# Scores by pairs of heads through a block-diagonal weight, and a fixed order of the first loads

## The chip, the cores and the metric

The kernel runs on one core of one Trainium2 chip. The metric is the device time of one execution in microseconds (us): 813.83 us is the median of three runs before the change (813.06 to 814.3). A core has a matrix engine (TensorE, PE in the profile, its weight loads PEld), three elementwise engines (VectorE is DVE, ScalarE is ACT, GpSimd is POOL) and SyncE (SP), which here only issues DMAs. Each engine runs its instructions in the order in which they were written for it, and waits at the first one whose inputs or buffer are not there. On-chip memory (SBUF) has 128 partitions; matmul results land in PSUM banks of 128 x 512 floats.

## The reference

There are 8 batches of 8 heads, 576 tokens, head width 64, and 32 memory slots per head. `phi` is `[8, 8, 576, 32]`.

```python
a   = softmax(phi, axis=2)                   # over the tokens
k_m = einsum('bhsm,bhsd->bhmd', a, k)        # 32 memory keys and values per head
v_m = einsum('bhsm,bhsd->bhmd', a, v)
scores = matmul(q, k_m^T) / sqrt(64)
x   = softmax(scores) @ v_m                  # then [8*576, 512]
out = relu(x @ w_in) ** 2 @ w_out            # 512 -> 2048 -> 512
```

All tensors are 32-bit floats, and the inputs q, k and phi are scaled so that the softmaxes are sharp; the kernel therefore keeps each large product as a sum of a high and a low part.

## The kernel before

**The work on one batch.** A batch is handled in two halves of four heads (`hh` = 0, 1). `memory(b, hh)` loads `phi`, k and v of four heads, takes the softmax over tokens, and multiplies into PSUM tile `pkv` (L426: four heads side by side, each in its own 32 columns of the array; 20 matmuls), sums (L439 for b < 2, L442 or L445 after that), and the reciprocal `rs`. From it come the transposed values `VTh`/`VTl` and the memory keys. `vw_step` and `vw_alone` multiply the values by w_in (`pvw`), so that `step` needs only the attention weights: `mm1` (L740) gives h, `mm2` (L770, L771, L773) multiplies the squared relu by w_out, and `mm2_left` (L796) does the last 64 tokens.

**Scores, batches 2 to 7.** `scores(b, hh)` loads q of two heads per DMA, 64 partitions of 18 x 64 floats (L557, two DMAs, 24 in all). The keys are scaled on ACT (`kvn`, L474), transposed 32 x 32 on DVE (`kT`, L477), and spread by a multiplication with the mask `bd` to a block weight `kb` of 2 x 128 columns (L562). q is transposed on DVE in two pieces of 8 and 10 token groups (`qT`, L569), and each piece is two matmuls over 128 partitions that add up in PSUM, one for each half of the head width (L574): 128 weights columns, 256 or 320 moving columns. DVE then transposes the scores back (L578), and the softmax follows.

**Scores, batches 0 and 1.** `first_attention` loads q by token rows (L602, 8 DMAs of 128 KB; the last 64 tokens by L595, tile `qx`), turns it on PE (L613), and multiplies by a block-diagonal key weight `kbd` of 128 x 128 (L636, L648). `kbd` comes from `kvx`, two DVE instructions (L459) that write keys and values twice beside each other under a parity mask, and a pair of PE transposes (L466).

**The weights.** w_in and w_out arrive as 64-bit pairs (`raw`, L322), are decoded to a high and a low part on DVE and ACT (L324 to L344) and for the first pieces on PE (`pd`, L350 to L352). w_in's parts are written to DRAM by POOL and loaded again as `wi` (L369) in later batches.

**What sets the order.** The kernel writes down all operations with an estimated duration on each engine they may use (`Plan.op`). `Plan.order` walks back from the due times of `mm2` (`cap`, set by `due`) to a latest start for each operation, and then fills the engines in time: an engine takes the ready operation whose latest start comes first, and preparatory work (`lead=True`) is taken 9 us (LEAD) ahead. The estimates also choose the engine where two are allowed. All loads go through one queue, SP. Of the loads of a batch the phi, k and v loads are two DMAs each (512 tokens, L377, and the last 64, L378).

## Time and profile before

| | |
|---|---|
| time, median of 3 (lowest, highest) | 813.83 us (813.06, 814.3) |
| the profiled execution: its own time; first to last instruction | 816.34 us; 814.6 us |
| PE busy | 776.2 us (95%) |
| DVE, ACT, POOL busy | 536.4, 403.1, 63.8 us |
| mean granted TensorE clock, first to last instruction | 0.994 |
| DMA packets, bytes | 99716, 101.04 MB |
| score matmuls L574, records and busy | 96, 27.6 us |

A row of a timeline has the start in us, the length, the engine, the line, the operation, the tile written and those read, and in brackets the idle time just before with what ended it. The length of a matmul includes its way through the array, so that lengths overlap: what a matmul takes from the next one is read from the starts. A 32-bit matmul of tiles that are not rounded appears as two records. A row of a table of windows has the stretch, its length, the busy time of PE, PEld, DVE, ACT and POOL with the number of instructions, the granted clock, the share of time that the DMA engines were busy and GB/s. SPq are the DMAs that SP issues.

### The profile page before, as it was taken

Reading aid. Unit: us, or ns where it says so; the run is one execution under the profiler, and the core shown is the slowest. Engines: PE = TensorE matmul, PEld = TensorE weight load, DVE = VectorE, ACT = ScalarE, POOL = GpSimd, SP = SyncE. Lnnn points to the kernel's source line nnn. Section 1 sums busy time; section 2 is a strip of 40 time slices with the busy share of each in tenths; the row PEclk is TensorE's granted clock in tenths of the full one; section 3 lists DMA queues with packets and bytes.
Section 4 is the critical chain, followed back from the end, with each engine's and each line's share of the span. In section 5 each row is a group of like instructions: output and inputs, shape, how many; then the busy total and the mean of one; then the engine's idle time right before and its main releaser. Section 6 shows DMA issues by size and latency. Waiting matters only on the chain.

```text
span 814.6 us, 13267 instructions
## 1 busy us (share of the span) xinstructions
PE 776.2 (95%) x4926; PEld 652.5 (80%) x4926; DVE 536.4 (66%) x1190; ACT 403.1 (49%) x922; POOL 63.8 (8%) x103
## 2 busy tenths in 40 slices
PE   4889999999999999999999999999999999999995
PEld 2567888778887888888778888888788888888884
DVE  4678888783468976766776556877677556864540
ACT  2557766675653465634445355644334355643220
POOL 4012202320100100010000100010000100000000
PEclk9999999999999999999999999999999999999998
DMA  7969967666456523423443433513422433100001
GB/s 225 270 191 286 270 176 239 188 170 191 125 146 189 165 81 105 129 37 90 132 125 88 126 106 104 136 34 91 133 58 70 122 108 104 30 24 29 1 1 64
DMA packets 99716, 101.04 MB, mean 124 GB/s; under 512 B 32260, under 2 KB 85508, under 8 KB 99652
## 3 DMA queue, kind: packets, MB, share of 16 engines
q1 hardware_dynamic: 89188, 81.55, 34.2%
q0 software_dynamic: 10464, 18.65, 8.8%
q8 instruction: 39, 0.64, 0.3%
q14 instruction: 25, 0.20, 0.1%
HBM read 79.17 MB, written 17.83 MB: 119 GB/s over the span
## 4 chain that ended last, share of the span: by engine, by line
PE 73%; DVE 8%; issue 6%; DMA 5%; ACT 4%; SPq 1%; POOL 1%; DVEq 0%; POOLq 0%; ACTq 0%
PE h L740 20%; PE acc L770 12%; PE acc L773 12%; PE acc L771 12%; PE accl L796 5%; PE pvw L536 4%; PE psc L574 3%; PE pkv L426 2%; DMA raw<-in_moe_w_out_dram 1%; DMA phi<-in_phi_dram 1%; ACT vw L260 1%; DMA raw<-in_moe_w_in_dram 1%; DMA wo<-work 1%; DVE glo L750 1%; DVE work L327 1%
## 5 line engine op out<-in xcount | busy, mean ns | idle before, releaser
L740 PE MATMUL h<-ath,vw 128*128 128x320 f32 (+1 forms) x1024 | 211.6, 298 | 1.1 <-ACT r L744 0.6
L770 PE MATMUL acc<-wo,gh 128*128 128x512 f32 x512 | 207.0, 404 | 1.8 <-ACT gh L746 1.6
L771 PE MATMUL acc<-wo,gh 128*128 128x512 f32 x512 | 201.7, 394 | 0.0
L740 PEld LDWEIGHTS h<-ath,vw 128*128 128x128 f32 x1024 | 171.0, 189 | 17.2 <-ACT r L744 1.7
L773 PE MATMUL acc<-wo,glo 128*128 128x512 f32 x512 | 162.1, 405 | 1.7 <-DVE glo L750 1.5
L260 ACT CAST vw<-pvw 64x256 fp32r<-64x256 f32 (+1 forms) x224 | 85.7, 397 | 74.5 <-PE pvw L536 35.4
L545 DVE TENSOR_TENSOR vw<-pvw,vw 64x256 fp32r<-64x256 f32 x192 | 78.8, 420 | 64.8 <-ACT vw L260 62.9
L770 PEld LDWEIGHTS acc<-wo,gh 128*128 128x128 f32 x512 | 96.4, 188 | 23.4 <-ACT gh L746 3.7
L740 PE MATMUL h<-atl,vw 128*128 128x320 f32 (+1 forms) x512 | 109.9, 295 | 0.0
L771 PEld LDWEIGHTS acc<-wo,gh 128*128 128x128 f32 x512 | 96.4, 188 | 16.6
L773 PEld LDWEIGHTS acc<-wo,glo 128*128 128x128 f32 x512 | 89.5, 189 | 19.5 <-DVE glo L750 6.2
L746 ACT ACTIVATE gh<-r 128x512 fp32r<-128x512 f32 x128 | 80.8, 632 | 43.4 <-DVE r L745 37.6
L750 DVE TENSOR_TENSOR glo<-r,gh 128x512 fp32r<-128x512 f32 x128 | 87.5, 684 | 21.4 <-ACT r L748 19.7
L744 ACT ACTIVATE r<-h 128x256 f32<-128x256 f32 (+1 forms) x149 | 60.1, 406 | 56.8 <-PE h L740 53.5
L745 DVE TENSOR_SCALAR r<-h 128x320 f32<-128x320 f32 (+1 forms) x107 | 48.9, 459 | 58.4 <-PE h L740 57.9
L740 PEld LDWEIGHTS h<-atl,vw 128*128 128x128 f32 x512 | 82.5, 189 | 0.7 <-issue 0.2
L747 ACT ACTIVATE gl<-r 128x64 fp32r<-128x64 f32 x128 | 32.8, 256 | 68.5 <-DVE r L745 66.5
L748 ACT ACTIVATE r<-r 128x576 f32<-128x576 f32 x94 | 64.5, 686 | 2.2
L796 PE MATMUL accl<-wo,gl 128*128 128x512 f32 x192 | 52.3, 397 | 0.1
L796 PEld LDWEIGHTS accl<-wo,gl 128*128 128x128 f32 x192 | 35.0, 188 | 7.2 <-DVE o L260 0.5
L536 PE MATMUL pvw<-wi,VTh 128*128 128x256 f32 x192 | 37.3, 286 | 0.6 <-issue 0.3
L749 DVE TENSOR_TENSOR r<-r 128x576 f32<-128x576 f32 x34 | 25.7, 756 | 15.8 <-ACT gh L746 14.4
(137 smaller groups left out, 854.3 us busy)
## 6 DMA issues: line engine op xcount, KB each, us to landing
wi<-w_in_hi SPq DMA_DIRECT2D x56, 256.0 KB
wi<-w_in_lo SPq DMA_DIRECT2D x56, 256.0 KB
KV<-in_k_dram SPq DMA_DIRECT2D x32, 256.0 KB
KV<-in_v_dram SPq DMA_DIRECT2D x32, 256.0 KB
raw<-in_moe_w_in_dram SPq DMA_DIRECT2D x16, 512.0 KB
raw<-in_moe_w_out_dram SPq DMA_DIRECT2D x16, 512.0 KB
q<-in_q_dram SPq DMA_DIRECT2D x24, 288.0 KB
out_dram<-o POOLq DMA_DIRECT2D x20, 256.0 KB, 7.7
```

The source lines that it names most:

```text
L260: nc.scalar.copy(o, i) if e == "ACT" else ENG[e].tensor_copy(o, i)
L536: nc.tensor.matmul(pw()[:, x * SL:(x + 1) * SL], l()[:, 2 * hh + x, :], w(r, x), start=(i == 0), stop=(i == 2))
L545: vec({"DVE": tt(SL)}, lambda e, V=V, pr=pr, src=src: nc.vector.tensor_sub(V()[pr, 1, hh, :], src(), V()[pr, 0, hh, :].bitcast(F32)), [pw, ...
L740: nc.tensor.matmul(p()[:, 0:n], V()[:, l, hh, c0:c0 + P], x()[:, hh, cs], start=(i == 0), stop=(i == 5))
L744: op({"ACT": act(n) - 30, **({} if b < 2 else {"DVE": tt(n)})}, lambda e, cs=cs, n=n, p=p: nc.scalar.activation(r()[:, cs], p()[:, 0:n], A ...
L746: op({"ACT": act(SM)}, lambda e: nc.scalar.activation(gh(), r()[:, 0:SM], AF.Square), [r], [gh])
L748: op({"ACT": act(S), **({} if b < 2 else {"DVE": tt(S)})}, lambda e: nc.scalar.activation(r(), r(), AF.Square) if e == "ACT" else nc.vecto ...
L750: vec({"DVE": tt(SM)}, lambda e: nc.vector.tensor_sub(glo(), r()[:, 0:SM], gh().bitcast(F32)), [r, gh], [glo])
L770: nc.tensor.matmul(a(), gh()[:, c], t()[:, 0], start=f0, stop=False)
L771: nc.tensor.matmul(a(), gh()[:, c], t()[:, 1], start=False, stop=False)
L773: nc.tensor.matmul(a(), glo()[:, c], t()[:, 0], start=False, stop=f1)
L796: nc.tensor.matmul(a(), G()[:, l, :], t()[:, w], start=(ff == 0 and n == 0), stop=(ff == NFF - 1 and n == 2))
```

## The change

It has two parts.

1. Batches 2 to 7 get their scores as the first two batches do, from a block-diagonal weight. `memory` now makes `kvx`, two PE transposes and `kbd` for every batch; the tiles `kvn`, `kT`, `vx` and `kb` and their instructions are gone. Each piece of q is still two matmuls, but one for each pair of heads: 64 weight columns, 256 or 320 moving columns, all 128 partitions, and the two stand in different halves of the array's columns (`tile_position=(0, 64 * y)`) and write different halves of the PSUM partitions. For that q must lie with two heads' halves of the head width on the partitions: each load now takes one head and half of its width, 32 x 18 pieces of 32 floats, eight DMAs in place of two (96 in place of 24). The planned durations of these steps are as before.
2. A list `FIRST` names the first loads in a fixed order, and gives each a `cap` far ahead of all others, so that the planner issues them in this order on SP.

```diff
+    def dma(fn, size, r=(), w=(), eng="SP", two=False, first=None, **more):
...
+        if first in FIRST:
+            more["cap"] = 10000 * FIRST.index(first) - 1e6
...
+    FIRST = ['phi 0 0', 'kv 0 0', 'phi 0 1', 'kv 0 1', 'wi 0', 'q 0 0', 'q 0 1', 'ql 0', 'wo 0']
...
-    kbd = kTs[b, hh] = st([P, P], F32, "kb", f"kbd{u}", 2)              # b < 2 only
+    kbd = kTs[b, hh] = st([P, P], F32, f"kb{b % 2}{hh}", f"kbd{u}")
...
-        Q = st([P, NC * D], F32, "q", f"q{u}")
-        for x in (0, 1):
-            h0 = 4 * hh + 2 * ((x + b) % 2)
-            dma(lambda d, x=x, h0=h0: d(Q()[64 * x:64 * x + 64], q[b, h0:h0 + 2].rearrange("h (p c) d -> (h p) (c d)", c=NC)),
-                2 * S * D * 4, [], [(Q, x)], lead=True)
+    def halves_of(d, dst, src):
+        for u in (0, 1):
+            d(dst[32 * u:32 * u + 32], src[:, 32 * u:32 * u + 32].rearrange("(p c) d -> p c d", c=NC))
...
+        Q = st([P, 2, NC, 32], F32, "q", f"q{u}")
+        for y in (0, 1):
+            for i in (0, 1):
+                hd = 4 * hh + (2 * (y + b) + i) % 4
+                dma(lambda d, y=y, i=i, hd=hd: halves_of(d, Q()[64 * i:64 * i + 64, y], q[b, hd]), S * D * 4, [], [(Q, (y, i))], two=True, lead=True)
...
-                for x in (0, 1):
-                    nc.tensor.matmul(pq()[:, 0:32 * n], kb()[:, x].rearrange("p h m -> p (h m)"),
-                                     qT()[:, x, 0:n].rearrange("p c t -> p (c t)"), start=(x == 0), stop=(x == 1))
+                for y in (0, 1):
+                    ys = slice(64 * y, 64 * y + 64)
+                    nc.tensor.matmul(pq()[ys, 0:32 * n], kbd()[:, ys], qT()[:, y, 0:n].rearrange("p c t -> p (c t)"),
+                                     start=True, stop=True, tile_position=(0, 64 * y))
```

The first place where rows move is SP's queue at the start of the program. The names are the tile and the tensor in DRAM that it is read from; `KV_1_0` and `KV_1_1` are keys and values of the second four heads of batch 0, `q_0` and `q_1` its queries. Before:

```order
L377 DMA phi_1_93<-in_phi_dram 128x4x128
L378 DMA phi_1_93<-in_phi_dram 64x4x32
L322 DMA raw<-in_moe_w_in_dram 128x2x512 x2
L377 DMA KV_1_0_140<-in_k_dram 128x2x256
L378 DMA KV_1_0_140<-in_k_dram 64x2x64
L377 DMA KV_1_0_140<-in_v_dram 128x2x256
L378 DMA KV_1_0_140<-in_v_dram 64x2x64
L377 DMA KV_1_1_167<-in_k_dram 128x2x256
```

And now:

```order
L382 DMA phi_1_93<-in_phi_dram 128x4x128
L383 DMA phi_1_93<-in_phi_dram 64x4x32
L382 DMA KV_1_0_115<-in_k_dram 128x2x256
L383 DMA KV_1_0_115<-in_k_dram 64x2x64
L382 DMA KV_1_0_115<-in_v_dram 128x2x256
L383 DMA KV_1_0_115<-in_v_dram 64x2x64
L382 DMA KV_1_1_143<-in_k_dram 128x2x256
L383 DMA KV_1_1_143<-in_k_dram 64x2x64
L382 DMA KV_1_1_143<-in_v_dram 128x2x256
L383 DMA KV_1_1_143<-in_v_dram 64x2x64
L327 DMA raw<-in_moe_w_in_dram 128x2x512 x2
```

The two loads of raw w_in have moved behind the eight loads of the second heads' keys and values; ahead of them and from the queries on the order is as before, but that the last queries (`qx`) now come ahead of raw w_out.

The second place is PE in the same stretch: `pmx` and `pkv` belong to `memory`, `pd` to the decoding of w_in. Before, from the last matmul of the first heads' `pkv` on:

```order
L350 MATMUL pd_0_206<-work,ident 128x512
L351 MATMUL pd_0_206<-wi_0_0_184,minus 128x512
L466 MATMUL pvt_0_190<-ident,kvx_0_182 128x128 x2
L352 MATMUL pd_0_206<-wi_0_0_184,minus 128x512
L411 MATMUL pmx_1_216<-ident,mx_1_143 128x128
L350 MATMUL pd_1_233<-work,ident 128x512
L414 MATMUL pmx_1_216<-ident,mc_1_222 128x128
L351 MATMUL pd_1_233<-wi_0_1_220,minus 128x512
L352 MATMUL pd_1_233<-wi_0_1_220,minus 128x512
```

And now:

```order
L470 MATMUL pvt_0_182<-ident,kvx_0_175 128x128 x2
L416 MATMUL pmx_1_193<-ident,mx_1_141 128x128
L419 MATMUL pmx_1_193<-ident,mc_1_196 128x128
L444 MATMUL pkv_1_217<-ones,phi_1_93 32x1 x20
L431 MATMUL pkv_1_217<-KV_1_0_115,phi_1_93 32x128 x2
...
L431 MATMUL pkv_1_217<-KV_1_1_143,phi_1_93 32x128 x2
L355 MATMUL pd_0_249<-work,ident 128x512
L356 MATMUL pd_0_249<-wi_0_0_215,minus 128x512
L431 MATMUL pkv_1_217<-KV_1_0_115,phi_1_93 32x128 x2
```

The second heads' memory now stands ahead of the decoding of w_in, though the last eight of its 20 matmuls stand between and behind the three `pd` matmuls of the first piece.

The third place is DVE where batch 2 gets its first keys. Before:

```order
L451 TENSOR_SCALAR rs_0_2380<-pkv_0_2113 128x1
L452 RECIPROCAL rs_0_2380<-rs_0_2380 128x1
L750 TENSOR_TENSOR glo_2384<-r_2329,gh_2345 128x512
L479 SCALAR_TENSOR_TENSOR vx_0_2395<-pkv_0_2113,rs_0_2380,par 128x128
L477 STREAM_TRANSPOSE kT_0_2398<-kvn_0_2393 128x64
L562 TENSOR_TENSOR kb_0_2402<-kT_0_2398,bd 128x256
```

And now:

```order
L556 STREAM_TRANSPOSE qT_0_0_2401<-q_0_2327 128x2x256
L739 TENSOR_TENSOR gl_1889<-r_2330,gl_1889 128x64
L456 TENSOR_SCALAR rs_0_2376<-pkv_0_2136 128x1
L457 RECIPROCAL rs_0_2376<-rs_0_2376 128x1
L463 SCALAR_TENSOR_TENSOR kvx_0_2387<-pkv_0_2136,rs_0_2376,par 128x128 x2
L738 TENSOR_TENSOR glo_2392<-r_2330,gh_2366 128x512
```

Three instructions (`vx`, `kT`, `kb`) have become two (`kvx`), and the transpose of the queries stands just ahead of them, where before three `glo` instructions with their `gl` lay between.

More of the change, by code (lines that the diff above doesn't have):

```diff
@@ L454, in memory @@
         halves = par.rearrange("p (r o) -> p r o", o=1)
-        if b < 2:
-            kvx = st([P, 2, 2, D], F32, "at", f"kvx{u}")
-            for i in (0, 1):
-                vec({"DVE": 300}, lambda e, i=i: nc.vector.scalar_tensor_tensor(
-                    kvx()[:, i], pk()[:, i * D:(i + 1) * D].rearrange("p (o d) -> p o d", o=1).broadcast_to([P, 2, D]), rs(),
-                    halves.broadcast_to([P, 2, D]), ALU.mult, ALU.mult), [pk, rs], [(kvx, i)], port=None, lead=True)
-            pv = pt("pa", f"pvt{u}")
-            def turn_kv(e):
-                for i in (0, 1):
-                    nc.tensor.transpose(pv()[:, i * P:(i + 1) * P], kvx()[:, i].rearrange("p r d -> p (r d)"), ident)
-            op({"PE": 450}, turn_kv, [kvx], [pv], lead=True, lat=300)
-            kbd = kTs[b, hh] = st([P, P], F32, "kb", f"kbd{u}", 2)
-            op({"ACT": act(P)}, lambda e: nc.scalar.copy(kbd(), pv()[:, 0:P]), [pv], [kbd], lead=True)
-            values(b, hh, pv, P)
-            return
@@ L484, in memory @@
[L484 to L487 removed]
+        kvx = st([P, 2, 2, D], F32, "kvx", f"kvx{u}")
+        for i in (0, 1):
+            vec({"DVE": 300}, lambda e, i=i: nc.vector.scalar_tensor_tensor(
+                kvx()[:, i], pk()[:, i * D:(i + 1) * D].rearrange("p (o d) -> p o d", o=1).broadcast_to([P, 2, D]), rs(),
+                halves.broadcast_to([P, 2, D]), ALU.mult, ALU.mult), [pk, rs], [(kvx, i)], port=None, lead=True)
+        pv = pt("pa", f"pvt{u}")
@@ L488, in values, with turn_kv @@
+        def turn_kv(e):
+            for i in (0, 1):
+                nc.tensor.transpose(pv()[:, i * P:(i + 1) * P], kvx()[:, i].rearrange("p r d -> p (r d)"), ident)
+        op({"PE": 450}, turn_kv, [kvx], [pv], lead=True, lat=300)
+        kbd = kTs[b, hh] = st([P, P], F32, f"kb{b % 2}{hh}", f"kbd{u}")
+        op({"ACT": act(P)}, lambda e: copy(e, kbd(), pv()[:, 0:P]), [pv], [kbd], lead=True)
         for s in (0, 1):
             ch = 2 * hh + ((s + b) % 2)
-            src = lambda s=s: pv()[:, at + 64 * s:at + 64 * s + 64]
+            src = lambda s=s: pv()[:, P + 64 * s:P + 64 * s + 64]
```

36 lines of the change are left out of this document (9 added, 27 removed).

## The prediction

> **What bounds the kernel now.** I read the chain of waits on the page first, in which PE has 73%, and then the busy time by stage.
>
> ```profile
> PE 73%; DVE 8%; issue 6%; DMA 5%; ACT 4%; SPq 1%; POOL 1%; DVEq 0%; POOLq 0%; ACTq 0%
> ```
>
> ```profile
> core 0 of [0], span 814.6 us
> core 0: us, PE busy (x) PEld busy (x) DVE busy (x) ACT busy (x) POOL busy (x), PEclk, DMA share, GB/s
> 0.00:20.00 20.00, 8.02 (x89) 4.26 (x90) 8.62 (x21) 5.37 (x11) 8.68 (x18) 1.00 0.79 226
> 20.00:40.00 20.00, 16.54 (x169) 11.90 (x169) 12.27 (x31) 11.01 (x21) 2.22 (x4) 1.00 0.98 269
> 40.00:60.00 20.00, 17.39 (x148) 12.36 (x148) 15.34 (x35) 11.21 (x25) 2.84 (x5) 0.91 0.67 188
> 200.00:800.00 600.00, 596.40 (x3657) 507.74 (x3657) 390.36 (x879) 278.46 (x659) 21.00 (x40) 1.00 0.33 93
> ```
>
> Between 200 and 800 us PE is busy 596.40 of 600 us, DVE 390, and the DMA engines a third of the time. There a microsecond of PE is a microsecond of the kernel, and nothing else counts until it makes PE wait; only 3.6 us of idle time are left to win. The first 60 us are another regime: PE is busy 41.95 us of 60, so 18 us are lost, and the waits of other engines and of the loads decide. The two parts of the change fall one in each stage.
>
> **Scores, batches 2 to 7: what is saved on PE.** How long a matmul holds PE is read from the starts.
>
> ```profile
> 248.06 0.27 PE L483 MATMUL pvt<-ident,vx 128*128 128x128 f32 x1
> 248.08 0.47 PE L770 MATMUL acc<-wo,gh 128*128 128x512 f32 x1
> 248.40 0.39 PE L771 MATMUL acc<-wo,gh 128*128 128x512 f32 x1
> ...
> 249.56 1.03 PE L574 MATMUL psc<-qT,kb 128*128 128x256 f32 x4
> 250.23 0.58 PE L770 MATMUL acc<-wo,gh 128*128 128x512 f32 x1
> 250.65 0.39 PE L771 MATMUL acc<-wo,gh 128*128 128x512 f32 x1
> ...
> 252.25 1.24 PE L574 MATMUL psc<-qT,kb 128*128 128x320 f32 x4
> 253.09 0.63 PE L770 MATMUL acc<-wo,gh 128*128 128x512 f32 x1
> 253.56 0.39 PE L771 MATMUL acc<-wo,gh 128*128 128x512 f32 x1
> 253.78 0.39 PE L770 MATMUL acc<-wo,gh 128*128 128x512 f32 x1
> ```
>
> A matmul of 512 columns holds PE 0.23 us (253.56 to 253.78). A score piece of 256 columns starts at 249.56; the L771 two places on starts at 250.65, and the L770 between took 0.23, so the piece held PE until 250.42: 0.86 us for four records, 0.215 each. The piece of 320 columns likewise: 253.56 - 0.23 - 252.25 = 1.08 us. The old scores of one half of a batch hold PE 1.94 us, the 12 halves 23.3 us. A PE transpose (L483) costs 248.40 - 248.06 - 0.23 = 0.11 us.
>
> Now each piece is two matmuls of 64 weight columns in two halves of the array. If they overlap fully a piece takes half, 0.43 and 0.54. Whether they do, and what the split array costs, the trace shows only for other shapes:
>
> ```profile
> 243.53 0.39 PE L773 MATMUL acc<-wo,glo 128*128 128x512 f32 x1
> 243.85 0.28 PE L445 MATMUL pkv<-ones,asum 128*64 128x1 f32 x4
> 244.07 0.50 PE L740 MATMUL h<-ath,vw 128*128 128x256 f32 x2
> 244.41 0.40 PE L740 MATMUL h<-atl,vw 128*128 128x256 f32 x2
> 244.64 0.40 PE L740 MATMUL h<-ath,vw 128*128 128x256 f32 x2
> 244.97 1.43 PE L426 MATMUL pkv<-KV,phi 128*32 128x128 f32 x40
> 246.34 0.96 PE L773 MATMUL acc<-wo,glo 128*128 128x512 f32 x3
> 247.13 0.40 PE L770 MATMUL acc<-wo,gh 128*128 128x512 f32 x1
> ```
>
> Overlap: L426 has 40 records of 128 columns, which at half of 0.215 each would take 4.3 us one after the other; they took 1.57 (three L773 end at 247.13, so they begin to stream at 246.44; the L740 pair before, 0.12 each by the starts of its rows, streams from 244.64 to 244.87). Its four column groups overlap: 40/4 x 0.107 = 1.07 us, and of the rest 0.50 us is no streaming. The same from L445, the only pair of 64 columns at this place: L773 streams to 243.76, the first L740 pair must begin at 244.41 - 0.23 = 244.18, so the pair with its one moving column cost 0.42, nearly all of it for going into and out of the split array; a record of one column is at most a few hundredths, so I take 0.36 for the way in and out. Then a piece of 256 costs 0.43 + 0.36 = 0.79, one of 320 costs 0.54 + 0.36 = 0.90: 0.07 and 0.18 us less, 0.25 per half, 3.0 us in all. Each `memory` of these batches has one PE transpose more (two `kvx` for one `vx`): 12 x 0.11 = 1.3 us back. **On PE: -1.7 us.** The bounds: with no cost of the split, -(23.3 / 2 - 1.3) = -10.3 us; with no overlap and that cost, 24 x 0.36 + 1.3 = +9.9 us. I stay near L445, which has the same split.
>
> [...]
>
> **Scores: the other engines.**
>
> Two DVE instructions of 128 columns take the place of three, and a copy of `kbd` on ACT that of `kvn`. With DVE busy 390 and ACT 278 of the 600 us neither bounds, so I count nothing.
>
> The queries cost more queue time: eight issues for two. Eight q issues of the opening stand in the row of 5.04 us quoted below, 0.63 each; so each load occupies SP 3.8 us longer and its end comes so much later. Behind it in the queue wait the next `wi`, k and v. The wire has room (share 0.33). What happens when DVE waits for q is in the trace:
>
> ```profile
> 196.71 0.71 DVE L569 STREAM_TRANSPOSE qT<-q 128x512 f32<-128x512 f32 x1 [4.33 <-DMA q<-in_q_dram]
> ```
>
> DVE stood still 4.33 us, longer than the 3.8, and PE's timeline has no idle time from 190 to 204 us. The transposes are planned ahead of need, and a wait of 3.8 us fits under that cover; at the first load of batch 2 three more `glo` now stand ahead of the transpose. I count nothing; without the cover six second loads, which cannot start before the tile is free, would cost 6 x 3.8 = 23 us. Nor do I count a gain of PE's few waits on `vx`.
>
> **The opening.**
>
> ```profile
> 8.57 1.11 SPq L322 DMA_DIRECT2D raw<-in_moe_w_in_dram  x2
> ...
> 16.06 0.61 SPq L378 DMA_DIRECT2D KV<-in_v_dram  x1
> 16.75 5.04 SPq L602 DMA_DIRECT2D q<-in_q_dram  x8
> ```
>
> ```profile
> 13.46 0.43 DVE L324 TENSOR_SCALAR work<-raw 128x512 f32<-128x512 f32 x1 [1.10 <-DMA raw<-in_moe_w_in_dram]
> ...
> 16.07 0.43 DVE L324 TENSOR_SCALAR work<-raw 128x512 f32<-128x512 f32 x1 [0.72 <-DMA raw<-in_moe_w_in_dram]
> ```
>
> ```profile
> 15.33 2.08 PE L350 MATMUL pd<-work,ident 128*128 128x512 f32 x2 [2.88 <-DVE work L327]
> ...
> 19.43 0.30 PE L411 MATMUL pmx<-ident,mx 128*128 128x128 f32 x1 [0.58 <-DVE VTl L494]
> ...
> 26.80 2.00 PE L636 MATMUL psc<-kbd,qT 128*128 128x64 f32 x16
> ```
>
> The two raw loads are issued eight DMAs later, 8 x 0.63 = 5.0 us (the pace of the q row): their data lands at 18.5 and 21.1 instead of 13.46 and 16.07. The last KV issue goes from 16.06 to 8.57 + 7 x 0.63 = 13.0. The memory of the second heads was not held up by its data before but by its place behind `pd` on PE (`pmx` at 19.43 only). Now it runs while raw is on the wire. But its last matmuls are behind `pd` again: the first piece's decoding reaches `pd` 1.9 us after landing as before (13.46 to 15.33), at 20.4; the third `pd` matmul needs DVE's L345, which stands behind the second piece's first instruction (21.1) and two more, so it comes at about 23 and `pkv` ends at 23.5, and then the second piece's `pd` and the turns of q lie before the scores `psc`, which come at about 27 as before (26.80). What is won at the first is lost at the second. **Opening: 0.** From both sides: at best all of the 3.0 us by which k and v come earlier, at worst the 5.0 us of raw.
>
> **Sum:** -1.7. The profiled execution has 816.34 us, of them 814.6 from first to last instruction; it would come to 814.6. It lies 2.5 above the median of the runs, so the same difference at the median gives 813.8 - 1.7 = 812.1, and I say **812.0**.
>
> **The rivals.** First, the opening becomes faster: DVE's idle time (7.7 of the 20 us from 20 on) speaks for it, the `pd` in between against: -1.7 - 3.0, 809.1. Second, slower: the raw loads bound the opening, for the chain of waits runs from SP's queue over raw to DVE L324 and `pd`. The price is 5.0 us at 13.46; it decides if `pvw` and w_in, and not the softmax of batch 0, come last at the first h. Against it: the softmax has DVE to share with the decoding up to 40 us whichever comes first. 813.8 - 1.7 + 5.0 = 817.1. Third, the halves of the array overlap without a price: 803.5; L445 speaks against it. Fourth, they do not overlap (+9.9, 823.7) or late queries stop PE (813.8 - 1.7 + 23, 835): the four groups of L426 and the wait at 196.71 speak against them. Fifth, the saving ends in other waits, since the order of all engines changes from 20 us on: 813.8.
>
> **How the numbers follow.** A time that differs by less than 0.2% (1.6 us) can't be told from no change. Forecast 0.42, half of it beyond that bound because the sum lies just on it; faster opening 0.20; raw bounds 0.17; free overlap 0.05; no overlap or late queries 0.08; saving lost 0.08. Faster: 0.21 + 0.20 + 0.05 = 0.46. Slower: 0.17 + 0.08 + 0.01 = 0.26. Same: the rest, 0.28. The range leaves out the free overlap, the fourth and some of the edges: 807.5 to 817.5. The forecast's own is 810.4 to 813.7.
>
> **What would show it.** In the new profile: score matmuls at 64 columns whose two groups start together, a piece holding PE about 0.79 and 0.90 us; 12 more transposes; PE busy from 200 to 800 us still above 99%; DVE waits for q without idle time on PE right behind; raw landing near 18.5 us and `psc` near 27. I am wrong if a piece holds PE less than 0.6 or more than 1 us, if PE's idle time before 60 us is not 18 but 14 or 22, or if PE waits for scores.

## The result, and the profile after

The change makes the kernel slower: 837.17 us (median of 4 executions, 834.87 to 843.51) against 814.07 us for the kernel before on the same chip (813.06 to 815.63). The ratio is 1.0294, with a 95% interval of 1.0233 to 1.0356. The profiled execution took 843.51 us, 841.8 of them from the first to the last instruction; it is the longest of the four, so what follows accounts for 27.2 us (841.8 - 814.6), where the medians differ by 23.1.

The chain of waits on the page of the changed kernel still has PE at the same share; what has grown are DMA (5 to 7%) and SP's queue (1 to 3%):

```profile
PE 73%; DVE 9%; DMA 7%; ACT 5%; SPq 3%; issue 2%; DVEq 0%; POOLq 0%; ACTq 0%
```

The same stretches as in the prediction, for the changed kernel (after the stretch and its length come the busy times of PE, PEld, DVE, ACT and POOL, then the granted clock, the DMA share and GB/s). Before, the stretch from 60 to 200 us had PE busy 132.82 us at clock 1.00:

```profile
0.00:20.00 20.00, 7.17 (x138) 4.76 (x142) 7.46 (x18) 4.07 (x7) 7.51 (x16) 1.00 0.77 218
20.00:40.00 20.00, 17.68 (x122) 11.46 (x113) 13.31 (x33) 10.82 (x22) 3.33 (x5) 0.94 0.97 277
40.00:60.00 20.00, 18.07 (x136) 12.61 (x137) 13.52 (x33) 9.44 (x22) 1.65 (x3) 0.72 0.67 191
60.00:200.00 140.00, 127.39 (x786) 106.66 (x785) 107.04 (x225) 92.73 (x197) 30.77 (x39) 0.96 0.67 199
200.00:800.00 600.00, 587.82 (x3609) 488.56 (x3609) 387.46 (x858) 276.55 (x659) 21.00 (x40) 0.99 0.37 97
```

Two things cost. PE is idle more: 841.8 - 790.2 = 51.6 us against 814.6 - 776.2 = 38.4, which is 13.2 us of the 27.2. And PE is busy 14.0 us longer (790.2 against 776.2) although it has less to do, because the granted clock falls to half (0.50) for stretches: two `pd` matmuls of L355 take 1.92 us at 97.65 us, in such a stretch, and 1.02 at 86.86 us. Half of PE's busy time in such a stretch is taken as its price (an estimate): 5.8 us from 37.7 to 51.4 us, 4.4 behind 95.8, 3.9 behind 290.3 and 1.7 behind 751.1 us, together 15.9, against 1.7 in the kernel before. The three dearest, each as the stretch with the idle time and the stretch behind it:

```profile
34.00:37.70 3.70, 2.11 (x10) 1.17 (x10) 3.56 (x8) 2.74 (x7) 0.00 (x0) 1.00 1.05 306
37.70:51.40 13.70, 11.68 (x30) 6.90 (x28) 10.72 (x23) 5.76 (x11) 1.18 (x2) 0.50 0.97 264
88.00:95.80 7.80, 2.35 (x13) 1.63 (x12) 3.24 (x9) 1.58 (x4) 0.00 (x0) 1.00 0.68 222
95.80:106.00 10.20, 8.82 (x32) 7.41 (x33) 6.83 (x16) 5.71 (x12) 3.39 (x4) 0.50 0.55 155
286.00:290.30 4.30, 0.71 (x5) 0.19 (x2) 4.13 (x9) 1.61 (x4) 1.08 (x2) 1.00 0.76 145
290.30:300.50 10.20, 7.81 (x29) 6.43 (x28) 5.78 (x13) 2.33 (x6) 0.00 (x0) 0.50 0.48 125
```

At the last two places PE is busy 8.82 and 7.81 us at half clock for what by this estimate takes 4.41 and 3.91 at full clock: each of these stalls is paid about a second time. (The half clock follows here on gaps of 5.71 and 3.59 us, shown below; in a later run it follows on two gaps of 1.50 and 1.26 us.)

**Where the time goes, by place.** The start of the n-th w_out matmul into the tile `acc` can be compared across traces. The table has, for some n, its time before and how much later (us) it starts in each profile; the kernels are those of the experiments below. A column is one execution, which can lie up to 7 us from the median of its kernel (843.51 against 837.17 for the changed one, 823.59 against 819.1 for the two queues).

| place before | changed | loads alone | loads, reload moved | scores alone | scores, order pinned | the same, two queues | changed, reload moved |
|---|---|---|---|---|---|---|---|
| 51 us | 3.4 | 3.4 | -0.1 | 0.5 | 4.7 | 5.9 | 4.0 |
| 121 us | 12.0 | 8.4 | -2.2 | -1.1 | 4.9 | 4.2 | 3.3 |
| 241 us | 13.4 | 8.8 | -0.7 | -3.0 | 3.3 | 2.0 | 5.5 |
| 280 us | 21.8 | 3.7 | -5.7 | 8.0 | 9.5 | 11.8 | 13.4 |
| 501 us | 22.6 | 5.0 | -4.5 | 9.6 | 10.9 | 9.8 | 14.2 |
| 543 us | 28.4 | 5.0 | -4.5 | 15.5 | 16.8 | 9.6 | 20.1 |
| 684 us | 24.0 | 4.5 | -5.2 | 11.0 | 12.4 | 7.7 | 15.7 |
| 726 us | 28.6 | 4.5 | -5.2 | 14.4 | 15.8 | 7.5 | 19.0 |
| 793 us | 27.2 | 4.4 | -5.3 | 13.2 | 14.5 | 6.8 | 17.7 |

The changed kernel loses time at about 90 us and at 280 us, and less at about 530 and 720 us, where part of the step is given back behind it because work only stands in another order. It is also 3.4 us late by 51 us, with the half clock from 37.7 us on. At 93 us the table's difference would be -1.8, but only because the work stands in another order than before: against the experiment with the last `accl` steps behind, which has the same order up to there and only 3.4 us of half clock in the opening, the changed kernel is 3.9 us late at 51 us and still 3.5 at 93. Four of the six profiles with these fixed loads have the stretch of 13.7 us, and none of the ten others; the two that lack it (`accl` behind, and loads with the reload moved) have the same opening. Whether the change brings it is therefore not shown.

**The place at 90 us** is in SP's queue. First the changed kernel, then the one before:

```profile
76.01 0.62 SPq L327 DMA_DIRECT2D raw<-in_moe_w_in_dram  x1
82.53 0.37 SPq L374 DMA_DIRECT2D wi<-w_in_hi  x1
83.00 0.63 SPq L327 DMA_DIRECT2D raw<-in_moe_w_in_dram  x1
83.74 0.52 SPq L374 DMA_DIRECT2D wi<-w_in_lo  x1
84.36 5.18 SPq L327 DMA_DIRECT2D raw<-in_moe_w_out_dram  x2
```

```profile
75.99 3.39 SPq L322 DMA_DIRECT2D raw<-in_moe_w_in_dram  x2
80.81 0.37 SPq L369 DMA_DIRECT2D wi<-w_in_hi  x1
81.28 0.41 SPq L369 DMA_DIRECT2D wi<-w_in_lo  x1
81.83 3.77 SPq L322 DMA_DIRECT2D raw<-in_moe_w_out_dram  x2
```

Before, both raw w_in loads were issued by 79.4 us. Now the second stands behind `wi<-w_in_hi`, the reload of a part of w_in that POOL must first have written to DRAM; SP waits for such writes, 5.6 us at the longest between 72 and 98 us (the profile names `w_in_lo<-wi`), and the raw load goes out at 83.00. DVE's decoding (L329) then waits for the raw data, first of w_in and then of w_out, and PE behind it:

```profile
87.47 0.43 DVE L329 TENSOR_SCALAR work<-raw 128x512 f32<-128x512 f32 x1 [2.87 <-DMA raw<-in_moe_w_in_dram]
...
94.47 0.43 DVE L329 TENSOR_SCALAR work<-raw 128x512 f32<-128x512 f32 x1 [4.56 <-DMA raw<-in_moe_w_out_dram]
```

```profile
97.17 0.69 PE L610 MATMUL pql<-ident,qx 128*128 128x128 f32 x2 [5.71 <-ACT qT L604]
```

**The place at 280 us** is the second load of queries of batch 2. The kernel before (SP, DVE and PE):

```profile
252.58 1.20 SPq L557 DMA_DIRECT2D q<-in_q_dram  x2
```

```profile
258.76 0.71 DVE L569 STREAM_TRANSPOSE qT<-q 128x512 f32<-128x512 f32 x1
```

```profile
259.53 1.13 PE L574 MATMUL psc<-qT,kb 128*128 128x256 f32 x4 [0.28 <-DVE qT L569]
```

The data landed at 258.67 (the DMA records), DVE turned it at once, and PE had already stood still 0.28 us for it: at this load there was no cover at all. The changed kernel:

```profile
265.22 5.31 SPq L537 DMA_DIRECT2D q<-in_q_dram  x8
```

```profile
279.45 0.71 DVE L556 STREAM_TRANSPOSE qT<-q 128x512 f32<-128x512 f32 x1
...
284.32 0.84 DVE L556 STREAM_TRANSPOSE qT<-q 128x640 f32<-128x640 f32 x1 [4.17 <-PE psc L562]
```

```profile
265.48 0.76 PE L562 MATMUL psc<-qT,kbd 128*64 128x320 f32 x4
...
283.62 0.65 PE L562 MATMUL psc<-qT,kbd 128*64 128x256 f32 x4
...
285.80 0.76 PE L562 MATMUL psc<-qT,kbd 128*64 128x320 f32 x4 [0.15 <-DVE S L566]
...
290.14 0.62 PE L523 MATMUL pvw<-wi,VTh 128*128 128x256 f32 x2 [3.59 <-issue]
```

The issues hold SP 4.1 us longer (5.31 against 1.20). The data lands at 272.70, 7.5 us after the first issue where it was 6.1. But DVE turns it only at 279.45, because other work stands ahead of it in DVE's order. (Where this order comes from is open. The planner now books 1.25 us for each pair of issues; but in the experiment with the old scores and the new loads, which leaves every planned duration as it was, the scores of the second heads stand late too. So a step behind the planner moves rows when the program is built.) The scores of the second heads stand 18 us behind those of the first (265.48 to 283.62; 7.3 before, 252.25 to 259.53), behind the left-over products (`accl`). With those done, PE has nothing left while DVE and ACT do the softmax, and stands still from 286.6 us.

**The score pieces** cost what the prediction said. In PE's timeline of the changed kernel:

```profile
262.31 0.40 PE L759 MATMUL acc<-wo,gh 128*128 128x512 f32 x1
262.63 0.65 PE L562 MATMUL psc<-qT,kbd 128*64 128x256 f32 x4
263.22 0.97 PE L761 MATMUL acc<-wo,glo 128*128 128x512 f32 x3
264.02 0.39 PE L758 MATMUL acc<-wo,gh 128*128 128x512 f32 x1
```

The L759 ahead streams until 262.54; the three L761 take 0.69, so the piece is through at 264.02 - 0.69 = 263.33: 0.79 us with the gap of 0.09 ahead of it. For 320 columns the same reading gives 0.89.

### The profile page after: what moved, and what is told of

The parts are those of the page before. It is cut to its first block, busy times and chain, and to the rows that moved or that the text cites. A ratio compares the mean times of both kernels' runs of the same rounds, so it can differ in the third digit from the quotient of the medians.

```text
span 841.8 us, 13409 instructions
## 1 busy us (share of the span) xinstructions
PE 790.2 (94%) x4938; PEld 650.8 (77%) x4938; DVE 540.1 (64%) x1185; ACT 399.6 (47%) x915; POOL 64.3 (8%) x103
## 2 busy tenths in 40 slices
DMA packets 154630, 101.06 MB, mean 120 GB/s; under 512 B 88708, under 2 KB 141956, under 8 KB 154564
## 4 chain that ended last, share of the span: by engine, by line
PE 73%; DVE 9%; DMA 7%; ACT 5%; SPq 3%; issue 2%; DVEq 0%; POOLq 0%; ACTq 0%
PE h L728 20%; PE acc L758 12%; PE acc L761 11%; PE acc L759 11%; PE accl L784 4%; PE pvw L523 4%; DMA raw<-in_moe_w_out_dram 3%; PE pkv L431 2%; PE psc L562 2%; SPq L382 1%; SPq L383 1%; PE pd L355 1%; PE pvw L503 1%; DMA raw<-in_moe_w_in_dram 1%; DMA phi<-in_phi_dram 1%
## 5 line engine op out<-in xcount | busy, mean ns | idle before, releaser
L728 PE MATMUL h<-ath,vw 128*128 128x320 f32 (+1 forms) x1024 | 216.2, 303 | 7.5 <-ACT r L732 2.2
L759 PE MATMUL acc<-wo,gh 128*128 128x512 f32 x512 | 202.2, 395 | 0.0
L728 PEld LDWEIGHTS h<-ath,vw 128*128 128x128 f32 x1024 | 173.4, 192 | 28.2 <-ACT r L732 4.8
L761 PE MATMUL acc<-wo,glo 128*128 128x512 f32 x512 | 160.4, 401 | 1.4 <-DVE glo L738 1.3
L728 PE MATMUL h<-atl,vw 128*128 128x256 f32 (+1 forms) x512 | 113.8, 300 | 0.3 <-DVE atl L695 0.2
L759 PEld LDWEIGHTS acc<-wo,gh 128*128 128x128 f32 x512 | 96.6, 189 | 17.3 <-issue 0.8
L761 PEld LDWEIGHTS acc<-wo,glo 128*128 128x128 f32 x512 | 89.2, 188 | 22.0 <-DVE glo L738 5.4
L733 DVE TENSOR_SCALAR r<-h 128x320 f32<-128x320 f32 (+1 forms) x113 | 51.3, 455 | 58.7 <-PE h L728 58.0
L732 ACT ACTIVATE r<-h 128x256 f32<-128x256 f32 (+1 forms) x143 | 57.8, 407 | 64.0 <-PE h L728 60.5
L728 PEld LDWEIGHTS h<-atl,vw 128*128 128x128 f32 x512 | 84.9, 193 | 2.9 <-DVE atl L695 1.0
L523 PEld LDWEIGHTS pvw<-wi,VTh 128*128 128x128 f32 x192 | 31.4, 190 | 8.7 <-issue 6.1
```

Of the source, the lines that this page charges most:

```text
L523: nc.tensor.matmul(pw()[:, x * SL:(x + 1) * SL], l()[:, 2 * hh + x, :], w(r, x), start=(i == 0), stop=(i == 2))
L728: nc.tensor.matmul(p()[:, 0:n], V()[:, l, hh, c0:c0 + P], x()[:, hh, cs], start=(i == 0), stop=(i == 5))
L732: op({"ACT": act(n) - 30, **({} if b < 2 else {"DVE": tt(n)})}, lambda e, cs=cs, n=n, p=p: nc.scalar.activation(r()[:, cs], p()[:, 0:n], A ...
L759: nc.tensor.matmul(a(), gh()[:, c], t()[:, 1], start=False, stop=False)
L761: nc.tensor.matmul(a(), glo()[:, c], t()[:, 0], start=False, stop=f1)
```

## The experiments

### Which of the two parts

Each ratio below is to executions of the kernel before on the same chip at the same time, whose medians were 814.32 to 817.81 us; so it is not the quotient with 814.07.

Each part alone, and of the scores the query loads alone. Loads alone (the kernel before with part 2):

```diff
-    FIRST = []
+    FIRST = ['phi 0 0', 'kv 0 0', 'phi 0 1', 'kv 0 1', 'wi 0', 'q 0 0', 'q 0 1', 'ql 0', 'wo 0']
```

> The kernel before with the second part of the change alone: the fixed order of the first loads. The order of PE is that of the changed kernel for the first 313 rows, some 130 us. If the start costs what its trace says (before 200 us PE has 4.5 us more idle time than in the kernel before and some 11 us more are lost to half clock), this kernel is 15 us slower, about 829, with the gap at 91.5 to 97.2 us and half clock from about 38 and from about 96 us. If the start costs nothing, as the prediction had it, it is at 814 and the whole loss belongs to the scores.

Measured: 821.49 us, ratio 1.0067 (1.0038 to 1.0096). Slower, though by only a third of what was expected, and at the same place as the changed kernel: the second raw w_in load is behind the reload again, and PE stands still 2.83 us at 88.1 and 1.99 at 93.2 us.

Scores alone (the changed kernel without part 2):

```diff
-    FIRST = ['phi 0 0', 'kv 0 0', 'phi 0 1', 'kv 0 1', 'wi 0', 'q 0 0', 'q 0 1', 'ql 0', 'wo 0']
+    FIRST = []
```

> The changed kernel without the fixed order of the first loads: the scores part alone. The first 320 rows of PE are those of the kernel before. If the stall at 286 us belongs to the scores part (8.6 us more idle time after 200 us, some 6 us of half clock, less 1.7 of saved work), it is 13 us slower, about 827, and a gap of 3 us or more with half clock behind it stands where the scores of batch 2's second heads are made. If the scores part does what the prediction said, it is at 812; if the loss is all in the start, at 812 to 814.

Measured: 830.18 us, ratio 1.0179 (1.0119 to 1.0239). In the profile nothing is lost up to 241 us (-3.0), then 11.0 us by 280, and 3.6 more from 501 us to the end; PE stands still 3.72 us at 271.5 and 3.32 at 276.6.

The old scores with the new loads: each of the two q loads of the kernel before is split into the four pieces of 32 partitions and 128-byte rows that the change has; matmuls and transposes stay.

```diff
+    def pieces(d, dst, src):
+        for h in (0, 1):
+            for u in (0, 1):
+                us = slice(32 * u, 32 * u + 32)
+                d(dst[32 * h:32 * h + 32, :, us], src[h, :, us].rearrange("(p c) d -> p c d", c=NC))
```

> The kernel before, its scores untouched, but each q load of batches 2 to 7 by eight DMAs of 128-byte rows in place of two of 4608-byte rows, to the same places. In the built order one thing moves: the scores of batch 2's second heads go behind nearly all of the left-over matmuls of batch 1. If the pieces of q are what makes the stall, this kernel has PE idle for 3 us or more at about 280 us with half clock behind it and costs 8 to 13 us (822 to 827), with DVE and PE work as before. If the stall comes from the new scores (kbd, pairs), this one stays at 814.

Measured: 834.93 us, ratio 1.0224 (1.0165 to 1.0283). The way of loading q, with the order that the build makes of it, costs by itself all that the scores cost; the new matmuls and transposes add nothing that can be told (1.0179 against 1.0224, with intervals that overlap). In the trace the order moves in later batches too: the scores that stood at 424 and 519 us before stand behind some 12 us more of other work.

The changed kernel with the last six steps of `accl` of batch 1 issued on PE only behind the scores of batch 2's second heads, so that PE has work while the softmax runs:

```diff
+    held = [accl[1, ff] for ff in range(10, NFF)]
...
+        if o in held:
+            with tc.issue_after(psc[2, 1, 1].ins):
+                o.fn(o.left)
```

> The changed kernel with one thing moved on PE: the last six of the sixteen left-over steps of batch 1 (accl, 18 matmuls, 4.1 us) are issued behind the scores of batch 2's second heads and not ahead of them. The other engines keep their order but for one copy on DVE. If PE stands at 286.6 to 290.1 because those scores come late and nothing else is left to do, the gap of 3.6 us and most of the 1.5 us after it go, and the half clock of 10 us behind it (some 4 us): 7 to 9 us faster than the changed kernel, 828 to 831. If PE waits there for something else (a late load of wi), the gap stays and the time is 837.

Measured: 832.05 us, ratio 1.0203 (1.0145 to 1.026) against 1.0294, with intervals that overlap. The gap of 3.59 us is gone and one of 1.80 is left; the half clock behind it lasts 3.4 us and not 10.2. So in the profile, idle time behind a scores step that comes late is part of the price. Only about a third of the 11.6 us between the two profiles is from there: from 241 to 320 us this kernel loses 6.0 us where the changed one loses 9.8. The rest is there by 121 us, where this profile has lost 3.9 us and that of the changed kernel 12.0, although the order is the same: 3.9 us of that difference lie before 51 us (3.4 us of half clock in place of 13.7), 4.2 at 90 us.

### Late data or late order

In the kernels with the new loads the scores of the second heads are both later in the order and later in their data. Two kernels have the old order of these steps put back on PE and DVE, and one has the old loads with the late order.

The old scores with the new loads and the order of before at batch 2's second heads; the scores alone with the same lines:

```diff
+        if o.left == "DVE" and at["qT", 2, 1, 0] < i <= at["psc", 2, 1, 1] + 30:
+            after = ins["qT", 2, 1, 0]
+        elif o in left[4:] and i > at["psc", 2, 1, 1]:
+            after = ins["psc", 2, 1, 1]
+        elif o in left[2:] and i > at["psc", 2, 1, 0]:
+            after = ins["psc", 2, 1, 0]
+        with tc.issue_after(after.ins) if after else nullcontext():
```

> The kernel before with the 128-byte pieces of q (as the run that cost 18 us), and with issue order pinned at one place: on DVE the work planned after the first transpose of q of batch 2's second heads is issued behind it, and on PE the left-over steps from the third on are issued behind the scores of these heads. At that place the order is then that of the kernel before. If the pieces cost time because the order was built with late queries, the stall of 2.6 and 4.3 us at 270 to 279 us and the half clock behind it go, and it is at 814 to 819 (up to 4 us stay for queries that really land 3 us later, and for batch 3). If the pieces cost time themselves, on SP's queue or on the wire, DVE waits for q at the pinned place, PE stands as long as before, and it stays at 828 to 834.

Measured: 830.9 us, ratio 1.0193 (1.013 to 1.0256), not told apart from 1.0224. Now the data itself stops PE. SP, DVE and PE of this kernel:

```profile
258.61 5.33 SPq L553 DMA_DIRECT2D q<-in_q_dram  x8
```

```profile
268.54 0.71 DVE L577 STREAM_TRANSPOSE qT<-q 128x512 f32<-128x512 f32 x1 [1.34 <-DMA wi<-w_in_hi]
```

```profile
269.30 1.13 PE L582 MATMUL psc<-qT,kb 128*128 128x256 f32 x4 [2.84 <-DVE qT L577]
```

The last q piece lands at 268.22, 9.6 us after the first issue against 6.1 before, and PE waits 2.84 us for it. (The wait of DVE is put down to `wi`, but the q landing at 268.22 is what came just ahead of 268.54.)

> The scores part of the change (pairs, 128-byte pieces, no fixed first loads) with the same pins for batch 2's second heads. If the order at that place is the whole loss, what is left is the prediction's own sum for the scores, -1.7 us, plus some 2 us of smaller waits of the later batches: 812 to 817. If the stall has another cause it stays near the 1.018 of the scores part alone, 829.

Measured: 826.78 us, ratio 1.0138 (1.0091 to 1.0184). Better than 1.0179, with overlapping intervals. The order explains a part at most.

The old loads with the late order: in the kernel before, 15 steps of `accl` are put ahead of the scores of the second heads.

```diff
+    ahead = [accl[1, ff] for ff in range(15)]
...
+        if o is scored[2, 1, 0]:
+            with tc.issue_after(left[1, 14].ins):
+                o.fn(o.left)
```

> The kernel before, with its two cheap q loads and old scores; only the order is made worse: fifteen of the sixteen left-over steps of batch 1 on PE are issued ahead of the scores of batch 2's second heads. If late scores in the order are what stops PE, this costs as much as the 128-byte pieces did: PE idle for 5 us or more after the scores, half clock for some 10 us behind it, 824 to 832. If the loss needs the pieces themselves, it stays at 814 to 817.

Measured: 821.89 us, ratio 1.0093 (1.0057 to 1.0129). With the queries on time the late order alone makes the stall: PE stands still 4.42 us ahead of `pvw`, with half clock for 6.8 us from 276.6 us on:

```profile
278.67 0.77 PE L536 MATMUL pvw<-wi,VTh 128*128 128x256 f32 x2 [4.42 <-issue]
```

The loss stays at 7.3 us to the end; there is no step at 530 us. So late order and late data each suffice for the step at 280 us, and undoing one alone gains little. That is why the first guess, that the order was the cause, did not hold.

The raw w_in data late at the start (the slower rival of the prediction): the fixed loads with raw w_in ahead of the second heads' k and v.

```diff
-    FIRST = ['phi 0 0', 'kv 0 0', 'phi 0 1', 'kv 0 1', 'wi 0', 'q 0 0', 'q 0 1', 'ql 0', 'wo 0']
+    FIRST = ['phi 0 0', 'kv 0 0', 'phi 0 1', 'wi 0', 'kv 0 1', 'q 0 0', 'q 0 1', 'ql 0', 'wo 0']
```

> The kernel before with a fixed order of the first loads in which the raw w_in stands ahead of the second heads' keys and values, where it was, and only the queries, the left-over queries and the first raw w_out have a fixed order behind them. The fixed order of the change cost 0.67%, 5.5 us. If raw w_in's later landing (18.5 in place of 13.5 us) is its price, this one is at 814 and PE's clock is at full speed from 19.4 us on, with 3.4 us or less of half clock at about 43 us. If the order behind it (w_out after the left-over queries) is the price, it is at 818 to 820.

Measured: 822.18 us, ratio 1.0109 (1.0072 to 1.0146). The raw data is decoded from 13.22 and 15.67 us on, as before the change, and the kernel is no faster than the one with the loads as in the change (1.0067). Bringing the raw data early takes no price away. But this kernel has a loss of its own that was not traced to a cause: on SP both raw w_in loads stand ahead of the reload, as before, and still PE stands 2.05 us at 85.1 us with 3.4 us of half clock behind it. That the late raw data is not the price is shown by the first experiment of the next group.

### Three that try to take the price away

The first reload of w_in, which waits on SP, put behind the next raw loads, in the kernel with the loads alone. Four rows of SP change places; the other engines keep their order.

```diff
+    first = [again[0, 0, 0, x] for x in (0, 1)]
     for o in plan.order():
-        o.fn(o.left)
+        with tc.issue_after(raws["wo", 3, 0].ins) if o in first else nullcontext():
+            o.fn(o.left)
```

> The kernel before with the fixed first loads (1.0067), and one thing moved on SP: the first reload of decoded w_in (two issues, that wait until POOL's stores have landed, at 82.7 us) goes behind the next raw w_in and the next raw w_out, which stand behind it in that kernel. No other engine's order differs in any row. If the price of the fixed first loads is that raw weights wait behind this reload and DVE, ACT and PE then wait for them (PE idle 2.8 and 2.0 us at 88 to 95 us), raw w_in is issued at about 80 in place of 83.2, the idle time goes down by 3 us or more, with less half clock behind, and it is at 1.000 to 1.003. If the price is paid earlier, by raw w_in's landing at 18.5 us or the clock before 51 us, it stays at 1.006.

Measured: 814.38 us, ratio 0.9989 (0.996 to 1.0019), from 1.0067. SP now issues both raw w_in loads and a raw w_out ahead of the reload:

```profile
72.48 4.51 SPq L329 DMA_DIRECT2D raw<-in_moe_w_in_dram  x2
80.27 0.34 SPq L329 DMA_DIRECT2D raw<-in_moe_w_out_dram  x1
80.90 0.37 SPq L376 DMA_DIRECT2D wi<-w_in_hi  x1
```

Its raw w_in is decoded from 18.86 and 20.99 us on, as late as in the change, and no difference from the kernel before can be measured: the late raw data costs nothing, the wait behind the reload was the whole price of the fixed loads, and there is nothing to win by them. From 51 to 121 us, which leaves the opening out, the table has +5.0 us for the loads alone and -2.1 with the reload moved.

The idle time behind the scores filled with work: the scores alone, with 60 matmuls of the identity with itself, whose result is not used, behind the scores of the second heads.

```diff
+                def busy(e, p=p):
+                    for i in range(60):
+                        nc.tensor.matmul(p()[:, 0:P], ident, ident, start=True, stop=True)
```

> The scores part alone (1.0179; PE idle 3.7 us at 271.5 and 3.3 us at 276.6, half clock from 275.6 to 285.8), with 60 transposes of the unit matrix, 6.6 us of PE, put behind the last scores of batch 2, where PE stands idle; their results are overwritten. If PE's idle time is what halves its clock, the stretch of half clock goes and the work behind it, some 7.5 us of busy time at half pace, takes 3.5 to 4 us less: 826. If the clock drops for another cause, it drops again and the time is 829 or more, since the filling delays the next matmuls.

Measured: 832.89 us, ratio 1.0213 (1.0152 to 1.0274), against 1.0179 without the filling. First the unfilled kernel's idle stretch and the one behind it, then the filling in PE's timeline and the filled kernel's stretch:

```profile
271.00:275.60 4.60, 0.88 (x7) 0.37 (x4) 3.68 (x8) 1.51 (x4) 0.00 (x0) 1.00 0.80 135
275.60:285.80 10.20, 6.15 (x26) 5.22 (x25) 6.09 (x14) 1.98 (x5) 0.00 (x0) 0.50 0.43 119
```

```profile
278.08 13.66 PE L729 MATMUL h<-ident 128*128 128x128 f32 x120
```

```profile
278.00:291.50 13.50, 13.50 (x122) 13.42 (x121) 9.32 (x19) 1.99 (x5) 0.00 (x0) 1.00 0.47 94
```

With PE kept busy the clock stays at 1.00: here the half clock comes from the idle time. But the filling took 13.66 us (0.23 for each matmul, which is two records, where 0.11 was counted), more than the idle time of 7.0 us and the 3.1 us lost at half clock that it replaced. It shows the clock's cause and does not show a gain.

The queries in half as many issues: each pair of 32-partition pieces in one DMA with the same 128-byte rows, in the kernel with the scores alone and the pinned order.

```diff
     def halves_of(d, dst, src):
-        for u in (0, 1):
-            d(dst[32 * u:32 * u + 32], src[:, 32 * u:32 * u + 32].rearrange("(p c) d -> p c d", c=NC))
+        d(dst, src.rearrange("(p c) (u d) -> u p c d", c=NC, u=2))
```

> The scores part with the pinned order (it stood at 1.0138), and each q load of batches 2 to 7 in four issues of 64 partitions in place of eight of 32; the 128-byte pieces are the same. In the pinned run on old scores the eight issues took 5.3 us of SP and the last landed 9.6 us after the first issue; the two old ones 1.2 and 6.1 us. If the queries are late because SP issues them one after the other, they land some 2.5 us earlier, PE's wait at the scores of batch 2's second heads shrinks under 1 us with no half clock behind it, and it is 5 to 8 us faster than with eight, 817 to 822. If the pieces' own time on the wire sets the landing, they land 9 us after the first issue again and it stays at 825 to 827.

Measured: 1001.47 us, ratio 1.227 (1.2185 to 1.2356), which no theory had foreseen. SP and PE at batch 2's second heads:

```profile
264.93 17.04 SPq L536 DMA_DIRECT2D q<-in_q_dram  x4
```

```profile
289.77 1.12 PE L563 MATMUL psc<-qT,kbd 128*64 128x256 f32 x4 [15.67 <-DVE rz_None L675]
```

Four issues hold SP 17.04 us, but not alike: the first takes 0.54 us, each of the next three 5.4 to 5.6, and the `wi` load behind them 5.29, against 0.66 for each of the eight. In the DMA records the 128-byte rows go out at about 212 per us, 5.4 us for the 1152 rows of one issue, and the DMA engines are busy 0.29 of the time from 264 to 282 us; with eight issues, in ten of the twelve loads of the changed kernel, the 4608 rows of a load take 5.5 to 6.7 us, 690 to 840 per us. So an issue behind the first holds SP about as long as one issue's rows take; whether it waits for the rows of the one before it is not shown. The bytes and the pieces are the same and the DMA records show no more packets (153188 in the whole kernel against 154630); what has changed is the shape of one issue, four dimensions for three on the DRAM side, with the two halves of the head width outermost. Why that is slow was not tried, and nothing is told by it on whether fewer issues would help.

### How much of it these causes explain

The changed kernel with the reload behind the raw loads (the lines of the experiment above):

> The changed kernel, with its first reload of w_in moved on SP's queue behind the next raw w_in and the next raw w_out; three SP rows differ, all other engines keep their order. Theory (in the changed kernel too, the price of the fixed loads is the raw weights that wait behind that reload, the 5.71 us of idle PE at 91.5 us and the half clock from 95.8 us on): the idle time goes, and the ratio to the kernel before falls from 1.029 to what the scores cost alone, 1.018 to 1.022. Rival (in the changed kernel the wait at 91.5 us has another cause, the first turn of the left-over queries or the wire): the ratio stays at 1.027 to 1.031.

Measured: 832.72 us, ratio 1.0212 (1.0183 to 1.0241). The idle time at 91 us shrinks from 5.71 to 1.18 us, the half clock from 95.8 us on is gone, and the profile loses 3.3 us and not 12.0 by 121 us. In the changed kernel too this is a price of the fixed loads (its interval just meets that of the change, 1.0233 to 1.0356; the half clock from 38.6 us on, 13.7 us long, stays).

The scores alone with the pinned order, and each query load issued half by SP and half by POOL:

```diff
-                dma(lambda d, ...: halves_of(...), S * D * 4, [], [(Q, (y, i))], two=True, lead=True)
+                dma(lambda d, ...: halves_of(...), S * D * 4, [], [(Q, (y, i))], eng="POOL" if i else "SP", two=True, lead=True)
```

> The kernel with the paired scores alone and the pinned order (1.0138), with four of the eight issues of each query load given to POOL's queue, four left on SP's; the pieces of 128 bytes stay. Theory (the loads are late because eight issues stand one after the other on one queue, 5.3 us): each load is issued 2.6 us sooner, lands about as much sooner, most of the waits for the scores go, and the ratio falls to 1.003 to 1.009. Rival (the pieces of 128 bytes are late on the way, not at the issue): the last piece lands as late as before and the ratio stays at 1.012 to 1.016. Second rival: POOL's issues cost more than SP's or stand behind stores that wait, and the ratio rises above 1.018.

Measured: 819.1 us, ratio 1.0057 (1.0027 to 1.0088), from 1.0138. The issues on SP now take 2.8 us and not 5.3. The ratio is where the theory had it. By the table the gain is in the later batches: from 501 us to the end the kernel with one queue loses 3.6 us, and this one gains 3.0. PE's idle time, 1.18 us from 500 to 560 and 1.77 from 700 to 760 us with one queue, is 0.06 and 0.03. Three things change together there: SP's time per load; the DMA records, 28416 fewer on SP's queue and only 2304 more on POOL's, which is 592 and 48 for each of the 48 issues of 576 rows, so that POOL's half no longer goes in rows of 128 bytes; and the order of PE and DVE (the scores that follow those of batch 2 start at 282.0 and not at 291.9 us). Which of them brings the gain is not shown. The step at 280 us stays. There the load takes as long as it did with one queue: the last piece issued by SP lands at 266.10, 7.4 us after the first issue (7.2 with one queue), and the DMA engines are busy nearly all of the time:

```profile
260.00:280.00 20.00, 16.95 (x84) 12.39 (x82) 18.23 (x38) 7.18 (x19) 6.83 (x12) 1.00 0.97 216
```

So at batch 2, where the queries share the DMA engines with k, v and the weights (DMA share 0.81 at this place with one queue, 0.56 in the kernel before), the load lands no sooner with fewer issues per queue. The windows around the idle time of this kernel:

```profile
276.50:281.00 4.50, 1.74 (x11) 1.21 (x10) 4.02 (x10) 2.09 (x5) 1.09 (x2) 1.00 0.86 230
281.00:287.80 6.80, 5.76 (x21) 3.15 (x20) 4.49 (x11) 0.84 (x2) 2.68 (x4) 0.50 0.52 127
```

The half clock (0.50 for 6.8 us) follows here behind gaps of no more than 1.50 us: two of them, 1.50 and 1.26, lie within 4 us, and in the 4.5 us ahead of it PE is busy for only 1.74.

The changed kernel with all three edits:

> The changed kernel with both edits: the reload behind the raw weights, and the pinned order with half of the query issues on POOL's queue. If the two causes are all there is, both prices go and the ratio is that of the kernel with the queries alone on two queues, within 0.005 of it. If something else in the changed order costs, it stays more than 0.008 above.

Measured: 822.41 us, ratio 1.0086 (1.0054 to 1.0118), within 0.003 of the scores alone with the same loads. The two causes take off 2.1 of the 2.9%. Of what is left, 7.2 us in the profile, 3.5 are there by 51 us, again with 13.7 us of half clock from 37.7 us on; 2.5 more come by 241 us and were not traced to a place, and 4.4 more by 280 us, at the same queries; some is given back later. A second q tile, which would let these loads start earlier, was not tried. No version beats the kernel before.

## Why the prediction was wrong

**What held.** The score pieces: 0.79 and 0.90 us were forecast, 0.79 and 0.89 measured, and 32 transposes (20 + 12). The saving of PE by itself stays below what the runs can tell: with the new query loads the new scores are ahead of the old ones by 2.0 us in the profiles (13.2 against 15.2), with the pinned order by 6.9 (14.5 against 21.4), and these differences hold other things too. The opening: raw data at 18.56 and 20.53 us (forecast 18.5, 21.1), the last issue of k and v at 13.04 (13.0), PE idle 17.1 us before 60 us (18; but 11.68 of PE's busy time there is at half clock, so less was done in it), and in PE's timeline

```profile
27.75 1.94 PE L624 MATMUL psc<-kbd,qT 128*128 128x64 f32 x16
```

where "about 27" was said. SP's part was right as well: 3.8 us longer per load was forecast, 4.1 measured.

**The step that failed: "a wait of 3.8 us fits under that cover".** It was read from the first load of batch 2, at 196.71 us, whose scores come only at 249.56, 53 us later. The second loads have no such cover: they cannot start before the tile is free. The row for that was in the trace of before: the q issue at 252.58, DVE's transpose at 258.76 right at the landing, and PE waiting 0.28 us for it. The prediction named the case without cover, "six second loads ... 6 x 3.8 = 23 us", and gave it a chance of 0.08 together with another; that the time worked out for it, 835 us, is near the 837.17 measured is luck. The scores alone cost 1.8% (14.6 us of the 814.07), and the six second loads don't pay alike: the step at the first is 11.0 us in the profile of the scores alone, all later ones together 5.2. The wait by itself was sized well: with the old scores and the order of before put back, PE waits 2.84 us at this place where it waited 0.28. What the sum of 3.8 for each load lacked is the order in which the scores then stand, the idle time behind them, and the half clock behind that.

**"Opening: 0"** was right for the place where it was looked for and wrong for the change. The sum followed the first 27 us. The fixed order also moved loads at 76 to 84 us on SP, and there a raw load slid behind a reload that waits for POOL's store: 0.67% alone (0.38 to 0.96), 5.5 us, about the bound of +5 that was set for another mechanism, the late raw data. That mechanism is refuted: with the raw data just as late and only the reload moved, the price is gone (0.9989). The order of SP at this place stands in the built program; the prediction compared the queue only up to the last k and v.

**"PE busy from 200 to 800 us still above 99%"**: 587.82 of 600, 98.0%. **The clock** was no term of the sum at all; 14.0 of the 27.2 us are longer busy time at half clock, 5.8 of them from 37.7 to 51.4 us, inside the opening that was put at nothing.

**The other rivals.** A faster opening did not come even with the reload moved (0.9989, interval through 1). Free overlap and no overlap of the two array halves are both excluded by 0.79 us. "The saving ends in other waits" is the nearest in kind of the small ones; it was priced at the saving of 1.7 us, where the scores alone cost 14.6.

**What stays open.** What makes the load at 260 us take 7 to 10 us from the first issue, against 6.1: the number of rows, their size of 128 bytes, or the other loads around it, since at this place all three changed together. Whether the fixed loads lengthen the half clock of the opening. Which step of the build puts the scores later. And the two prices, 0.67 and 1.79%, make 2.5, where the change cost 2.94 (2.33 to 3.56): a third price is neither shown nor excluded.

## What to carry to other kernels

Cover is a property of one load, not of a kind of load: of every load in a loop, look at the one whose buffer comes free last, and read from PE's row behind it how much time there was. When the order of a queue is changed at one end, compare the whole queue and look for a load that has slid behind one that waits for a store. And where PE is busy 99% of the time, a stall of some microseconds can be paid about twice, as those of 5.71 and 3.59 us here: once as idle time and once at half clock (4.4 and 3.9 us by the estimate above).

## What the runs showed of the hardware

- A q load as eight issues of 32 partitions x 18 rows of 128 bytes holds SP 0.66 us per issue. With the same bytes as four issues with one more dimension, the first holds it 0.54 us and each one behind it 5.4 to 5.6 (17.04 for the four), while the rows go out at 212 per us in place of 690 to 840.
- The stretches of half clock lasted 3.4 us (43.2 to 46.6 us in the kernel before), 6.8 (two queues, 281.0 to 287.8), 10.2 and 13.7 (the changed kernel), each about a multiple of 3.4. Like gaps cost very differently: after 3.82 us of idle time at 87.9 us it lasted 3.4 us in the kernel with the last `accl` steps behind, after 5.71 us at 91.5 us 10.2 us in the changed kernel, which has the same order there. So single profiles with the same work at one place can differ there by several us.
- At the start PE ran at half its later pace, though the windows have 1.00 there: two `pd` matmuls take 2.08 us at 15.33 us in the kernel before and 1.10 at 20.03. The first full clock came at different times, also without the fixed loads (19.4 us in the kernel before, 31.4 and 38.7 in the two with the scores alone and the pinned order, on one and on two queues). The kernels without the fixed loads have the same opening, and by 51 us those of the table lie 0.5 to 5.9 us behind the kernel before (4.7 with full clock from 31.4 us on, 5.9 from 38.7 on), which must not be put down to the edit.
